# Reordering a ramp on ScalarE, moving a temporary to another buffer pool, and adding seven fp32 matmuls ahead of a cumulative sum

## The chip, the cores and the metric

The kernel runs on one core of a Trainium2 chip. The metric is the device time of one execution in microseconds (us). The kernel before takes 323.64 us in the first set of runs (median of 3, 323.56 to 323.77).

The engines are named as in the profile: PE is TensorE (matmuls), ACT is ScalarE (activation functions and table loads), DVE is VectorE, POOL is GpSimd. Each engine has its own queue of instructions, and in the timelines below what stands behind a waiting instruction in the same queue waits too: in the changed kernel, for instance, one small ScalarE instruction waits 1.46 us for its operand, and the table load behind it starts only at 48.30.

## The reference, cut to what matters

The kernel computes a gated linear recurrence ("gateloop" attention) with a complex decay, and then a gated feed-forward layer on its output.

```python
batch, n_heads, seq, head_dim = (4, 8, 768, 48)
mag = np.sqrt(a_re * a_re + a_im * a_im)
scale = np.minimum(mag, 0.999) / (mag + 1e-06)
a_re_n, a_im_n = (a_re * scale, a_im * scale)
for t in range(S):                        # S_re, S_im: 48 x 48 states for each head
    new_re = ar * S_re - ai * S_im
    new_im = ar * S_im + ai * S_re
    S_re, S_im = (new_re + kv, new_im)    # kv = outer(k_t, v_t)
    y[:, :, t] = np.einsum('bhd,bhde->bhe', q[:, :, t], S_re)
# then, with x = y as 3072 x 384:
gelu = 0.5 * g * (1.0 + erf(g * inv_sqrt2))     # g = x @ w_gate
ffn_out = gelu * (x @ w_val) @ w_out
out = x + res_gate * ffn_out                    # res_gate = sigmoid(x @ w_res)
```

The kernel replaces the loop over time by cumulative sums in log space. For each position it needs the log magnitude of the decay and its angle (an arctan). Both are summed along the sequence by a matmul with a triangular matrix. `exp` of the one and `sin`/`cos` of the other then scale q and k.

## The kernel before

The sequence of each batch is cut into groups of 256 positions, 12 groups in all. They are worked on in units: `[0]`, `[1, 2]`, `[3, 4]`, and so on. "The second unit" is groups 1 and 2, "the third unit" groups 3 and 4. The ramp is the stretch in which the first units' decays are computed while the feed-forward layer has hardly any input yet.

The parts that matter, in the order in which the data pass through them. Comments marked `##` are mine, `...` marks cuts.

```python
    def p1_steps(g):
        def s0():
            ...
            act(out=T["lm", g], in_=T["lm", g], func=AF.Ln)                     ## tile "ar"
        def s1():
            T["s", g] = pS.tile([128, W], FP, tag="s", name="s")                ## pS: 2 buffers
            act(out=T["s", g], in_=T["lm", g], func=AF.Exp, scale=-1.0)
            nc.vector.tensor_tensor(out=T["th", g], in0=T["s", g], in1=T["th", g], op=OP.mult)
        def s2():
            act(out=T["s", g], in_=T["th", g], func=AF.Square)
        def s3():
            act(out=T["s", g], in_=T["s", g], func=AF.Ln, bias=1.0)
            lm = T["lm", g]
            nc.vector.scalar_tensor_tensor(out=lm, in0=T["s", g], scalar=0.5, in1=lm, op0=OP.mult, op1=OP.add)
            nc.vector.tensor_scalar(out=lm, in0=lm, scalar1=LNMAX, scalar2=None, op0=OP.min)   ## "the clamp"
        return [s0, s1, s2, s3]

    def cs_l(g, c):            ## running sum of the log magnitudes; psM: 4 PSUM buffers
        ...
        cs = psM.tile([128, DM], FP, tag="mm", padded_shape=[128, 512], name="csl")
        nc.tensor.matmul(out=cs, lhsT=lmat[c], rhs=T["lm", g][:, sl], start=True, stop=True)
        def ex():              ## "the exponentials": they free the PSUM buffer
            act(out=T["E", g][:, sl], in_=cs, func=AF.Exp)
            act(out=T["Ei", g][:, sl], in_=cs, func=AF.Exp, scale=-1.0)
        return ex

    def cs_t(g, c):            ## running sum of the angles: "cst"
        ...
        cs = psM.tile([128, DM], FP, tag="mm", padded_shape=[128, 512], name="cst")
        nc.tensor.matmul(out=cs, lhsT=tmat[c], rhs=th[:, sl], start=True, stop=(s == 0))
        if s > 0:
            nc.tensor.matmul(out=cs, lhsT=ones2pi, rhs=T["P", g], start=False, stop=True)
        ...                    ## VectorE turns cs into the tile fg (pool pE, 2 buffers); p2_sin takes Sin of it

    def sums(g):               ## per-head sums, for M = exp(sum), the decay over a whole block
        ms = psM.tile([128, H], FP, tag="mm", padded_shape=[128, 512], name="ms")
        two = pS.tile([128, W], FP, tag="s", name="two")
        ...
        for h in range(H):
            nc.tensor.matmul(out=ms[0:DD, h:h + 1], lhsT=two[:, h * DD:(h + 1) * DD], rhs=ones1,
                             start=(h == 0), stop=(h == H - 1), skip_group_check=True)
        T["ms", g] = mp.tile([128, H], FP, tag="ms", name="msb")
        nc.vector.tensor_copy(out=T["ms", g][0:DD], in_=ms[0:DD])
```

The order of all this in the ramp is set by one call of a helper, which sorts steps by a number between 0 and 1:

```python
        if u == 0:             ## g1: second unit, g2: third unit
            sm = [[call(sums, g) for g in gg if g % NS > 0] for gg in (g1, g2)]
            weave((0.0, 0.25, zip_steps([p1(g) for g in g1])), (0.26, 0.3, csls), (0.31, 0.32, sm[0]), (0.35, 0.45, exs),
                  (0.4, 0.64, zip_steps([p1(g) for g in g2])), (0.641, 0.642, dec3), (0.645, 0.65, atn[:1]),
                  (0.65, 0.66, [call(p1_arctan, g) for g in g1]), (0.67, 0.85, cst), (0.75, 0.8, atn[1:]),
                  (0.9, 0.95, sin), (0.96, 0.97, sm[1]), (0.0, 0.5, att))
```

So the queue of ScalarE has, in order: log and exp of the second unit, its exponentials (the last pair behind the first log of the third unit), log and exp of the third unit, the small `M` exponentials, a table load, the arctans, later the sines, another table load, and the GELUs of the feed-forward layer.

## Time and profile before

Over the whole span TensorE is the busiest engine. These are the first line of the page's busy times and the line of its chain that ended last (the share of the span that each engine has in it):

```profile
PE 272.1 (84%) x2200; PEld 170.5 (53%) x2200; DVE 234.8 (73%) x431; ACT 209.8 (65%) x353; POOL 80.5 (25%) x115
PE 56%; SPq 12%; ACT 11%; DMA 9%; DVE 6%; issue 3%; POOL 1%; ACTq 0%; DVEq 0%; POOLq 0%
```

These averages say little about the ramp, where the change lies. The timeline of ScalarE does. Its columns are start in us, duration in us, engine, source line, operation, output and input tile, shapes, count, and in brackets the idle time before with what ended it. L124 is the helper through which every activation goes, so one reads the tile names: E and Ei are the second unit's exponentials, `ar<-ar` the two logs with which the third unit begins, `M<-msb` the block decays, `ai<-ai` the arctans, CS the sines, h the GELUs.

```profile
36.59 0.49 ACT L124 ACTIVATE E<-csl 128x384 f32<-128x384 f32 x1 [0.91 <-PE csl L212]
...
39.52 0.84 ACT L124 ACTIVATE ar<-ar 128x768 f32<-128x768 f32 x1
...
42.05 0.85 ACT L124 ACTIVATE ar<-ar 128x768 f32<-128x768 f32 x1
...
47.74 0.29 ACT L124 ACTIVATE M<-msb 96x8 f32<-96x8 f32 x2
48.05 1.28 ACT L477 ACT_TABLE_LOAD   x1
49.34 3.04 ACT L124 ACTIVATE ai<-ai 128x768 f32<-128x768 f32 x4
57.58 0.94 ACT L124 ACTIVATE CS<-fg,hpi 128x768 bf16<-128x768 f32 x1 [5.20 <-DVE fg L246]
...
65.02 0.66 ACT L124 ACTIVATE h<-gp 128x256 bf16<-128x256 f32 x2
```

The timeline of TensorE in the same stretch (one fp32 matmul is two records, so "x16" are the eight one-column sums of one group and "x2" is one matmul of 384 columns):

```profile
39.21 1.44 PE L296 MATMUL ms<-ones,two 128*96 128x1 f32 x16
...
50.24 1.65 PE L236 MATMUL cst<-ai,lt0b 128*128 128x384 f32 x2 [7.84 <-ACT ai L124]
51.68 1.49 PE L238 MATMUL cst<-P,ones2pi 128*128 128x384 f32 x2
...
56.86 0.81 PE L238 MATMUL cst<-P,ones2pi 128*128 128x384 f32 x2
57.51 1.44 PE L296 MATMUL ms<-ones,two 128*96 128x1 f32 x16
58.81 0.49 PE L439 MATMUL gp<-xT,wg 128*128 128x256 bf16 x3
```

TensorE is idle for 7.84 us before the first cst matmul, and that matmul waits for the arctan. From one start to the next the early cst matmuls take 1.28 us and the late ones 0.65 us, because the granted clock changes between them, from 0.50 to 1.00. The table by windows shows it: after the stretch come busy us (and counts) of PE, PEld, DVE, ACT and POOL, then the granted TensorE clock, the DMA share and GB/s.

```profile
54.00:56.00 2.00, 2.00 (x7) 1.09 (x6) 1.28 (x3) 0.00 (x0) 0.00 (x0) 0.92 1.65 136
64.00:66.00 2.00, 1.11 (x14) 0.86 (x12) 1.86 (x5) 1.67 (x4) 0.00 (x0) 0.64 1.25 233
```

In every clock record of these traces the clock is either 0.5 or 1.0, so a mean of 0.92 in two microseconds tells when it changed. It is low from 44.1 to 54.3 and again from 64.6 to 71.4: by the trace's clock records for 10.24 and for 6.83 us. At the low clock a cst matmul takes 1.28 us against 0.65 us, about twice as long. Below I call what runs at 0.5 cold and what runs at 1.0 warm.

Last, VectorE (`msb` copies the sums out of PSUM, kE is the product of k and Ei, the last line is the clamp of group 4). Later I also name the updates, which are the additions just before the clamps, G and Gb, the running state times M and its bf16 copy, and P, the angle carried over from the group before:

```profile
40.69 0.16 DVE L299 COPY msb<-ms 96x8 f32<-96x8 f32 x1 [1.07 <-PE ms L296]
...
42.72 0.95 DVE L314 TENSOR_TENSOR kE<-k,Ei 128x768 bf16<-128x768 f32 x1
...
51.01 0.55 DVE L198 TENSOR_SCALAR ar<-ar 128x768 f32<-128x768 f32 x1
```

| ramp of the kernel before | us |
|---|---|
| TensorE idle before the first cst | 7.84 |
| first arctan | 49.34 |
| first cst to first Sin | 50.24 to 57.58 |
| first GELU | 65.02 |
| next table load, and the one that opens the last unit | 83.52 and 262.65 |

The last row is a milestone: how late a kernel reaches the same table load says what the ramp cost.

### The profile page before, as it was taken

How to read it: one execution, taken by the hardware profiler on the slowest of the kernel's cores; microseconds unless marked ns; L12 is line 12 of the kernel's file. 1: busy time of each engine (PE TensorE's matmuls, PEld its weight loads, DVE VectorE, ACT ScalarE, POOL GpSimd, SP SyncE). 2: the span in 40 equal slices, each digit the busy share in tenths (PEclk: the TensorE clock that was granted, in tenths of full speed). 3: DMA queues.
4: the chain of work that ended last, by engine and by line, in shares of the span. 5: the costliest groups of instructions: out<-in, count | busy, mean ns of one | idle time of the engine just before them, and what ended most of it. 6: DMA issues, size and time to landing. Idle time of an engine off the chain costs nothing.

```text
span 322.4 us, 5853 instructions
## 1 busy us (share of the span) xinstructions
PE 272.1 (84%) x2200; PEld 170.5 (53%) x2200; DVE 234.8 (73%) x431; ACT 209.8 (65%) x353; POOL 80.5 (25%) x115
## 2 busy tenths in 40 slices
PE   0337927789887999789997999998999999899994
PEld 0116624677543666445664556554656655555682
DVE  2446769968499995599982999974899837864352
ACT  4549684646998557977568976569665683656150
POOL 1206522022040370259020572000630003200220
PEclk9995676959999999999999999999999999999998
DMA  8999999989999995396850595000360003600441
GB/s 159 218 183 181 182 169 165 185 174 180 187 179 186 223 160 33 76 197 113 122 36 2 107 121 95 2 0 3 75 122 3 2 0 76 122 2 0 107 91 50
DMA packets 137755, 34.55 MB, mean 107 GB/s; under 512 B 126848, under 2 KB 137728, under 8 KB 137728
## 3 DMA queue, kind: packets, MB, share of 16 engines
q1 hardware_dynamic: 103296, 23.60, 36.8%
q0 software_dynamic: 34432, 10.59, 31.2%
q8 instruction: 17, 0.28, 0.3%
q14 instruction: 10, 0.08, 0.1%
HBM read 31.31 MB, written 9.07 MB: 125 GB/s over the span
## 4 chain that ended last, share of the span: by engine, by line
PE 56%; SPq 12%; ACT 11%; DMA 9%; DVE 6%; issue 3%; POOL 1%; ACTq 0%; DVEq 0%; POOLq 0%
PE vp L443 14%; PE gp L439 13%; SPq L136 6%; SPq L144 6%; PE op L463 6%; DMA k<-in_k_dram 4%; PE rp L455 3%; PE tp L349 3%; PE tp L346 3%; PE at L356 3%; ACT L477 3%; DMA m<-dm 3%; ACT s L124 3%; PE cst L236 2%; PE y L394 2%
## 5 line engine op out<-in xcount | busy, mean ns | idle before, releaser
L124 ACT ACTIVATE h<-gp 128x512 bf16<-128x512 f32 (+1 forms) x84 | 44.5, 536 | 38.4 <-PE gp L439 37.9
L439 PE MATMUL gp<-xT,wg 128*128 128x512 bf16 (+1 forms) x252 | 65.4, 353 | 3.4 <-ACT h L124 2.0
L443 PE MATMUL vp<-xT,wv 128*128 128x512 bf16 (+1 forms) x252 | 66.6, 353 | 0.0
L446 DVE SCALAR_TENSOR_TENSOR h<-h,vp 128x512 bf16<-128x512 bf16 (+1 forms) x84 | 49.8, 603 | 16.4 <-PE vp L443 12.0
L463 PE MATMUL op<-wo,h 128*128 128x384 bf16 x288 | 50.2, 326 | 8.1 <-ACT Ei L124 5.9
L463 PEld LDWEIGHTS <-h 128*128 128x128 bf16 x288 | 27.8, 98 | 28.7 <-issue 11.3
L351 ACT COPY qk<-tp 96x512 bf16<-96x512 bf16 x48 | 27.9, 580 | 17.1 <-PE tp L349 7.9
L359 DVE TENSOR_TENSOR atm<-at,mask 128x512 bf16<-128x512 f32 x48 | 32.9, 686 | 8.2 <-PE at L356 7.8
L472 POOL DMA_DIRECT2D out_dram<-x x22 | 20.4, 947 | 54.4 <-DMA out_dram<-ot 43.1
L439 PEld LDWEIGHTS <-wg 128*128 128x128 bf16 x252 | 23.7, 99 | 17.9 <-issue 4.2
L443 PEld LDWEIGHTS <-wv 128*128 128x128 bf16 x252 | 23.8, 99 | 13.3
L189 DVE TENSOR_TENSOR ai<-s,ai 128x768 f32<-128x768 f32 x12 | 11.1, 955 | 23.6 <-ACT s L124 23.6
L477 ACT ACT_TABLE_LOAD x21 | 26.9, 1283 | 1.1 <-PEq L615 0.7
L346 PE MATMUL tp<-ident,Q 128*96 128x128 bf16 x192 | 20.1, 231 | 6.9 <-DVE Q L321 6.2
L346 PEld LDWEIGHTS <-Q 128*96 128x96 bf16 x192 | 17.4, 130 | 15.3 <-DVE Q L321 10.0
L124 ACT ACTIVATE CS<-fg,hpi 128x768 bf16<-128x768 f32 x12 | 11.2, 935 | 20.8 <-DVE fg L246 20.7
L150 POOL DMA_DIRECT2D v<-in_v_dram x24 | 21.9, 932 | 4.2 <-DMA v<-in_v_dram 1.3
L349 PE MATMUL tp<-ident,K 128*96 128x128 bf16 x192 | 22.3, 235 | 0.0
L236 PE MATMUL cst<-ai,lt0b 128*128 128x384 f32 x24 | 11.8, 577 | 11.7 <-ACT ai L124 11.0
L352 DVE COPY qk<-tp 96x512 bf16<-96x512 bf16 x48 | 19.8, 413 | 2.3 <-ACT qk L351 1.7
L212 PE MATMUL csl<-ar,lt0a 128*128 128x384 f32 x24 | 11.4, 562 | 10.8 <-DMA ar<-in_a_re_dram 10.8
L466 DVE SCALAR_TENSOR_TENSOR ot<-sg,op 128x384 f32<-128x384 f32 x24 | 13.1, 547 | 10.1 <-PE op L463 10.1
(85 smaller groups left out, 522.0 us busy)
## 6 DMA issues: line engine op xcount, KB each, us to landing
ar<-in_a_re_dram SPq DMA_DIRECT2D x24, 192.0 KB, 4.7
ai<-in_a_im_dram SPq DMA_DIRECT2D x24, 192.0 KB, 4.1
q<-in_q_dram SPq DMA_DIRECT2D x24, 192.0 KB, 3.8
k<-in_k_dram SPq DMA_DIRECT2D x24, 192.0 KB, 3.7
out_dram<-ot SPq DMA_DIRECT2D x24, 192.0 KB, 2.5
out_dram<-x POOLq DMA_DIRECT2D x22, 192.0 KB, 3.7
v<-in_v_dram POOLq DMA_DIRECT2D x24, 96.0 KB, 5.0
wg<-in_moe_w_gate_dram POOLq DMA_DIRECT2D x4, 288.0 KB, 11.4
```

Of the source, the lines that this page charges most:

```text
L124: tab(nc.scalar.activation(**kw))
L150: nc.gpsimd.dma_start(out=t[:, c], in_=rows(v, g, c))
L346: nc.tensor.transpose(out=tp[0:DD, j * 128:j * 128 + 128], in_=Q(x), identity=ident)
L349: nc.tensor.transpose(out=tp[0:DD, 512 + j * 128:640 + j * 128], in_=K(x), identity=ident)
L351: nc.scalar.copy(out=qk[0:DD, 0:512], in_=tp[0:DD, 0:512])
L359: nc.vector.tensor_tensor(out=atm, in0=at, in1=mask4, op=OP.mult)
L439: nc.tensor.matmul(out=gp, lhsT=wg[:, fi, ffi * 128:(ffi + 1) * 128], rhs=xT[:, fi, :], start=(fi == 0), stop=(fi == KD - 1))
L443: nc.tensor.matmul(out=vp, lhsT=wv[:, fi, ffi * 128:(ffi + 1) * 128], rhs=xT[:, fi, :], start=(fi == 0), stop=(fi == KD - 1))
L446: nc.vector.scalar_tensor_tensor(out=h2[:, ffi, :], in0=h2[:, ffi, :], scalar=0.5, in1=vp, op0=OP.mult, op1=OP.mult)
L463: nc.tensor.matmul(out=ps, lhsT=h2[:, ffi, jj * 128:(jj + 1) * 128], rhs=wo[:, ffi, :], start=(ffi == 0), stop=(ffi == KF - 1))
L472: nc.gpsimd.dma_start(out=out[t0:t0 + 128, :], in_=T["x", token(u, jj)], accum_op=OP.add)
L477: tab(nc.scalar.preload_act_table_set(nm))
```

## The change

The intent, as I read it: ScalarE has small gaps between 33 and 41 us; the third unit's log and exp work can fill them if it goes ahead of the second unit's exponentials (all of it except the last logs, `p12[-2:]`, which stay behind them). And if TensorE has something to do in the idle stretch before cst, its clock may be up when cst comes. The whole diff:

```diff
@@ def cs_t(g, c):
         cs = psM.tile([128, DM], FP, tag="mm", padded_shape=[128, 512], name="cst")
+        if g == FIRST + 1 and c == 0:
+            for _ in range(7):
+                nc.tensor.matmul(out=cs, lhsT=tmat[1], rhs=T["lm", NEAR][:, sl], start=True, stop=True)
         nc.tensor.matmul(out=cs, lhsT=tmat[c], rhs=th[:, sl], start=True, stop=(s == 0))
@@ def sums(g):
-        two = pS.tile([128, W], FP, tag="s", name="two")
+        two = pE.tile([128, C * H, 2, D], FP, tag="fg", name="two").rearrange("p x u d -> p (x u d)")[:, 0:W]
@@ in the ramp
-            weave((0.0, 0.25, zip_steps([p1(g) for g in g1])), (0.26, 0.3, csls), (0.31, 0.32, sm[0]), (0.35, 0.45, exs),
-                  (0.4, 0.64, zip_steps([p1(g) for g in g2])), (0.641, 0.642, dec3), (0.645, 0.65, atn[:1]),
+            p12 = zip_steps([p1(g) for g in g2])
+            weave((0.0, 0.25, zip_steps([p1(g) for g in g1])), (0.26, 0.3, csls), (0.31, 0.32, sm[0]), (0.32, 0.5, p12[:-2]),
+                  (0.5, 0.58, exs), (0.6, 0.64, p12[-2:]), (0.641, 0.642, dec3), (0.645, 0.65, atn[:1]),
```

`NEAR` is group 4 and `FIRST + 1` is group 1. The result of the seven matmuls is thrown away, since the next one into the same PSUM buffer has `start=True`. Their operand, the log magnitude of group 4, is ready after the clamp of that group.

## The prediction

> **What bounds the kernel now.** Before takes 323.64 us. The page shows TensorE busy 84% of the span and 56% of the chain that ended last, but the change touches only the ramp, 32 to 72 us, where the latencies of ScalarE, VectorE and TensorE follow each other. In the timeline ScalarE runs Exp and Ln until 47.8, loads a table (1.28 us) and starts the first arctan at 49.34. TensorE is idle from 42.4 to 50.24 (7.8 us, ended by that arctan). Eight fp32 matmuls (cst, 128x384) follow: six at 1.28 us, or less as the clock rises, then 0.65 us each; the last ends at 57.7. VectorE then releases Sin at 57.58, Q starts at 59.53, and the first GELU runs at 65.02. Per-microsecond windows show a granted clock of 0.50 from 44.1 to 54.3 and again from 64.5 to 71.4. [...]
>
> **What the change moves.** ScalarE has small idle gaps from 33 to 41 us (0.84, 0.52, 0.91, 0.25, 0.55 us). The third unit's two Ln and two Exp (about 0.75 us each) fill them; the eight exponentials (0.38 us apart) then run without waits after the squares. Walking the built order with the trace's durations I get the first arctan at about 48.3 instead of 49.34: a gain of about 1 us. Taking the "two" tiles from another pool removes waits for the s buffers.
>
> **What it adds.** Seven fp32 matmuls of 0.65 us (4.5 us) to 1.28 us (9 us). The built order has them directly before the cst matmuls, waiting for the last clamp of the third unit's log magnitudes. On VectorE that clamp stands behind kE, two updates, G, Gb and P. I expect it at 51.5 to 52.1 us, later than the arctan that cst needs, so none of the seven fills the idle 7.8 us: all are on the critical path. They start cold; about four run at 1.28, three at 0.65: some 6.5 to 7 us. Cst then starts near 59 (before: 50.24), all warm (5.2 us, saving about 2), and ends near 64 instead of 57.7.
>
> Second cost: "two" now reuses an fg buffer, so the last sums wait for the first Sin pair, TensorE's gate and value matmuls queue behind those sums, and Q behind their copy: 1 to 2 us more. The first GELU should come near 71 (65.0 before).
>
> Giving back: if the clock stays up, or recovers sooner, after the GELU, up to 2.6 us of the second cold stretch returns. After that, to 102 us, the work is bound by TensorE and then ScalarE, so the delay passes through.
>
> **Sum.** About -1 (ScalarE) +6.7 (seven matmuls) +1.5 (later trigger) -2 (warm cst) +1.5 (fg buffer and order) -1 (later clock) = +5.7 us.
>
> Predicted: 329.3 us, range 325.0 to 333.0. Faster by over 2%: 0.03; within 2%: 0.57; slower by over 2%: 0.40.
>
> **What the profile would show.** Right: Ln of the third unit near 32.6 us; first arctan near 48.3; the extra matmuls starting after the clamp, at 51 to 53, with the first cst matmul waiting for them and not for the arctan; clock 1.0 during cst; the third sums after the first Sin. Wrong: the seven matmuls inside the idle stretch before the arctan, or cst at or before 50.
>
> **What would make it wrong.** [...] the seven run mostly warm, with the clock kept through 72 us: near 325. VectorE reaching the clamp much earlier, so that they overlap the arctan wait: 322 to 324. Or slack later (loads, stores) absorbing the delay.

That about four of the seven would run cold was my estimate; in the trace of before the clock rose 4.1 us after the first cst had begun (50.24 to 54.3), the time of three such matmuls at 1.28 us.

## The result, and the profile after

| | median us | lowest to highest | runs |
|---|---|---|---|
| before | 323.63 | 323.56 to 323.77 | 4 |
| after | 333.51 | 332.11 to 334.66 | 4 |

The ratio is 1.0303 (95% interval 1.0263 to 1.0343): slower by 3%. All these runs are fast (none is over 1.5% above the fastest of its kernel). Here and below a ratio is the mean time of one kernel's fast runs over that of the other's of the same rounds, so it is not quite the ratio of the medians quoted. The profile shown is of the fastest of the four runs after the change, 332.11 us. The median time lies half a microsecond above the predicted range, and the class that I held likeliest (within 2%, 0.57) did not come.

ScalarE after the change:

```profile
32.52 1.58 ACT L124 ACTIVATE ar<-ar 128x768 f32<-128x768 f32 x2
...
41.95 0.47 ACT L124 ACTIVATE E<-csl 128x384 f32<-128x384 f32 x1
...
48.07 0.21 ACT L124 ACTIVATE M<-msb 96x8 f32<-96x8 f32 x1 [1.46 <-DVE msb L302]
48.30 1.28 ACT L480 ACT_TABLE_LOAD   x1
49.59 3.04 ACT L124 ACTIVATE ai<-ai 128x768 f32<-128x768 f32 x4
65.28 0.94 ACT L124 ACTIVATE CS<-fg,hpi 128x768 bf16<-128x768 f32 x1 [12.64 <-DVE fg L249]
...
75.18 0.66 ACT L124 ACTIVATE h<-gp 128x256 bf16<-128x256 f32 x2
```

The third unit's logs start at 32.52 instead of 39.52, as intended. But the second unit's exponentials start at 41.95 instead of 36.59, and the arctan comes no earlier than before (49.59 against 49.34): a new wait of 1.46 us for a small copy on VectorE stands in front of the table load.

TensorE after the change (L238 are the seven matmuls):

```profile
42.85 2.01 PE L299 MATMUL ms<-ones,two 128*96 128x1 f32 x16 [3.47 <-ACT Ei L124]
45.12 2.72 PE L299 MATMUL ms<-ones,two 128*96 128x1 f32 x16 [0.25 <-DVE msb L302]
...
53.60 6.60 PE L238 MATMUL cst<-ar,ut0b 128*128 128x384 f32 x14 [5.42 <-issue]
60.04 0.81 PE L239 MATMUL cst<-ai,lt0b 128*128 128x384 f32 x2
...
68.08 2.69 PE L299 MATMUL ms<-ones,two 128*96 128x1 f32 x16 [2.72 <-DVE two L296]
70.63 0.80 PE L442 MATMUL gp<-xT,wg 128*128 128x256 bf16 x3
```

The seven matmuls do not lie in the stretch before the arctan. They start at 53.60, four microseconds after the first arctan began, and hold the first cst matmul until 60.04. The profile gives their wait to "issue", which here means that it saw no releaser; the clamp on VectorE that makes their operand ends at 52.96 + 0.55 = 53.51. Also new is a gap of 2.72 us before the third group of sums, which then takes 2.69 us instead of 1.44.

VectorE:

```profile
44.90 0.16 DVE L302 COPY msb<-ms 96x8 f32<-96x8 f32 x1 [3.74 <-PE ms L299]
...
47.88 0.16 DVE L302 COPY msb<-ms 96x8 f32<-96x8 f32 x1 [1.91 <-PE ms L299]
...
48.49 0.95 DVE L317 TENSOR_TENSOR kE<-k,Ei 128x768 bf16<-128x768 f32 x1
...
52.96 0.55 DVE L198 TENSOR_SCALAR ar<-ar 128x768 f32<-128x768 f32 x1
...
66.98 0.96 DVE L296 TENSOR_TENSOR two<-ar 128x768 f32<-128x768 f32 x1 [0.21 <-ACT CS L124]
```

It now waits 3.74 and 1.91 us for the sums, so kE comes at 48.49 instead of 42.72 and the clamp at 52.96 instead of 51.01. The last line is the tile `two` of the third sums: it waits for the sine, because it now sits in a buffer of the fg tag.

The clock, by windows (columns as before):

```profile
56.00:58.00 2.00, 2.00 (x5) 1.05 (x4) 0.00 (x0) 0.00 (x0) 0.00 (x0) 0.67 1.32 180
66.00:68.00 2.00, 0.00 (x0) 0.00 (x0) 1.75 (x4) 0.95 (x2) 0.00 (x0) 0.89 0.86 164
74.00:76.00 2.00, 1.34 (x20) 1.25 (x20) 1.27 (x2) 1.14 (x3) 1.31 (x2) 0.90 1.40 235
```

The clock rises at 57.3, falls at 67.6 in the gap of 2.72 us, and rises again at 74.4. The cst matmuls run warm, as was hoped (0.65 us from start to start). The sums (2.69 us), the gate and value matmuls and the first transposes that follow them run cold, at 0.50 until 74.4.

| | before | after | difference |
|---|---|---|---|
| first arctan | 49.34 | 49.59 | +0.25 |
| first cst | 50.24 | 60.04 | +9.80 |
| first Sin | 57.58 | 65.28 | +7.70 |
| first GELU | 65.02 | 75.18 | +10.16 |
| next table load | 83.52 | 91.72 | +8.20 |
| table load of the last unit | 262.65 | 270.64 | +7.99 |

### The profile page after: what moved, and what is told of

Its sections match the earlier page's. It is cut to its first block, busy times and chain, and to the rows that moved or that the text cites. A ratio compares the mean times of both kernels' runs of the same rounds, so it can differ in the third digit from the quotient of the medians.

```text
span 330.3 us, 5853 instructions
## 1 busy us (share of the span) xinstructions
PE 276.2 (84%) x2189; PEld 175.4 (53%) x2214; DVE 233.9 (71%) x431; ACT 209.3 (63%) x353; POOL 81.9 (25%) x115
## 4 chain that ended last, share of the span: by engine, by line
PE 57%; ACT 14%; DVE 11%; DMA 8%; issue 6%; SPq 2%; POOL 1%; DVEq 0%; ACTq 0%; POOLq 0%
PE gp L442 12%; PE vp L446 12%; PE op L466 4%; PE rp L458 4%; PE tp L349 4%; ACT s L124 3%; PE tp L352 3%; PE at L359 3%; ACT L480 3%; DMA m<-dm 3%; PE ms L299 2%; PE cst L239 2%; PE cst L238 2%; PE y L397 2%; PE dk L389 2%
## 5 line engine op out<-in xcount | busy, mean ns | idle before, releaser
L442 PE MATMUL gp<-xT,wg 128*128 128x512 bf16 (+1 forms) x241 | 63.4, 350 | 2.9 <-ACT h L124 1.1
L446 PE MATMUL vp<-xT,wv 128*128 128x512 bf16 (+1 forms) x238 | 61.8, 350 | 0.6 <-DVE ot L469 0.3
L171 POOL COPY landed<-k 1x1 f32<-1x1 f32 x10 | 7.1, 714 | 64.5 <-DMA k<-in_k_dram 64.5
## 6 DMA issues: line engine op xcount, KB each, us to landing
wg<-in_moe_w_gate_dram POOLq DMA_DIRECT2D x4, 288.0 KB, 10.6
```

The source lines that it names most:

```text
L442: nc.tensor.matmul(out=gp, lhsT=wg[:, fi, ffi * 128:(ffi + 1) * 128], rhs=xT[:, fi, :], start=(fi == 0), stop=(fi == KD - 1))
L446: nc.tensor.matmul(out=vp, lhsT=wv[:, fi, ffi * 128:(ffi + 1) * 128], rhs=xT[:, fi, :], start=(fi == 0), stop=(fi == KD - 1))
```

## The experiments

My theory: the loss is made in the ramp. The seven matmuls wait for the clamp of group 4, which lies behind the arctan, so all of them stand before cst; the new buffer of `two` adds a gap that costs the clock; and the new order on ScalarE gains nothing. One rival: the seven are cheap or useful, because they warm the clock for cst, and the order on ScalarE or the buffer makes the loss. Another rival: it is their number that costs, wherever they stand.

All experiments give correct results.

### no_fill: the change without the seven matmuls

```diff
-        if g == FIRST + 1 and c == 0:
-            for _ in range(7):
-                nc.tensor.matmul(out=cs, lhsT=tmat[1], rhs=T["lm", NEAR][:, sl], start=True, stop=True)
```

> The changed kernel without the seven matmuls. Theory 1 (the seven stand on the critical path): the first cst matmul starts with the arctan near 49.6 us, the second waits for P near 53.0, the rest run from there partly at half clock; the second cst group ends near 57, the first Sin near 59.5 instead of 65.3, the time falls by 4 to 6 us to 327.5 to 329.5. Rival (the cost is the moved log/exp work, whose sums run late and on a slow clock, and the seven cost little or help by keeping the clock up): the time stays within 1.5 us of 333.5 or rises.

Measured: 326.76 us (326.52 to 326.83, 4 runs), ratio to before 1.0070 (1.0047 to 1.0093). Taking the seven away gives back some 2.3% of the 3.0%. So the first rival falls: the seven are the larger part of the loss. The time fell even below the 327.5 to 329.5 us expected. But 0.7% (2.3 us) is left. In my sum the parts that stay in this kernel are -1 us for ScalarE and +1.5 us for the buffer. The profile shows where the rest goes, on TensorE:

```profile
45.33 2.72 PE L296 MATMUL ms<-ones,two 128*96 128x1 f32 x16 [0.25 <-DVE msb L299]
50.70 1.65 PE L236 MATMUL cst<-ai,lt0b 128*128 128x384 f32 x2 [2.31 <-ACT ai L124]
53.10 1.65 PE L238 MATMUL cst<-P,ones2pi 128*128 128x384 f32 x2 [0.76 <-DVE P L224]
...
63.38 1.49 PE L296 MATMUL ms<-ones,two 128*96 128x1 f32 x16 [2.62 <-DVE two L293]
```

The second cst matmul waits for P, a sum that stands behind the late kE and clamps in VectorE's queue, and the third sums wait for `two`.

### only_fill: the kernel before with the seven matmuls alone

```diff
         cs = psM.tile([128, DM], FP, tag="mm", padded_shape=[128, 512], name="cst")
+        if g == FIRST + 1 and c == 0:
+            for _ in range(7):
+                nc.tensor.matmul(out=cs, lhsT=tmat[1], rhs=T["lm", NEAR][:, sl], start=True, stop=True)
```

> The kernel before with only the seven matmuls. Theory 1: they start after the third unit's last clamp near 51.6 us, hold cst back to 57.5 to 59 (50.2 before), and the first GELU moves by 5 to 7 us; time 327.5 to 330.5. Rival (the seven cost little): cst all on the full clock and the time within 1.5 us of 323.6.

Measured: 332.40 us (331.53 to 334.10, 4 runs), ratio 1.0252 (1.0213 to 1.0290). With the old order the seven start at 52.50 and the first cst at 58.97. The milestone of the last unit is 6.1 us late (268.76). The profiled run, the slowest of the four, loses another 3.8 us at the end; see "A slow tail" below. The time lies above the 327.5 to 330.5 us expected; without that tail it would lie within (an estimate: 332.4 - 3.8 = 328.6). At the milestone, before the tail, the seven alone cost 6.1 us or 1.9%; taking them out of the change gives back 2.3%.

### only_fg: the kernel before with `two` in an fg buffer alone

```diff
-        two = pS.tile([128, W], FP, tag="s", name="two")
+        two = pE.tile([128, C * H, 2, D], FP, tag="fg", name="two").rearrange("p x u d -> p (x u d)")[:, 0:W]
```

> The kernel before with only the other buffer for two. If the reuse of an fg buffer costs on the critical path: the third sums start after the first Sin pair (near 60 us, 57.5 before), the first Q starts near 61.8 instead of 59.5, the first GELU moves by 1.5 to 2.5 us, time 325 to 326. If the reuse is off the path: the same time within 0.5 us.

Measured: 325.47 us (323.76 to 325.80, 6 runs), ratio 1.0038 (1.0011 to 1.0066), about 1.2 us. The third sums wait 2.72 us for `two` as in the change, but here the cold stretch that follows is short (61.8 to 65.2), and the profiled run, the fastest of the six, is even 0.7 us ahead of before at the last milestone. So this part costs little by itself.

### early_fill12: the kernel before with twelve matmuls that are ready early

```diff
+        if g == FIRST + 1 and c == 0:
+            for _ in range(12):
+                nc.tensor.matmul(out=cs, lhsT=tmat[1], rhs=T["lm", FIRST + 1][:, sl], start=True, stop=True)
```

> The kernel before with twelve matmuls on the second unit's log magnitudes, which are ready at 36.6 us, so they can start in the idle stretch near 42.4 and end near 50.1 at 0.645 us each. If warm filling in the idle stretch is worth anything: the clock stays 1.0 from 37 through 57 us, the eight cst matmuls take 5.2 instead of 7.4 us, the first Sin moves 1.5 to 2 us earlier, and the time is 321.5 to 323. If the clock falls in spite of them or cst is not what Sin waits for: 323.5 or more.

Measured: 325.45 us (325.19 to 327.15, 4 runs), ratio 1.0042 (1.0008 to 1.0077). In the ramp it does what the change meant to do. On TensorE:

```profile
42.12 7.96 PE L238 MATMUL cst<-ar,ut0b 128*128 128x384 f32 x24
50.14 0.91 PE L239 MATMUL cst<-ai,lt0b 128*128 128x384 f32 x2
...
59.36 0.42 PE L349 MATMUL tp<-ident,Q 128*96 128x128 bf16 x4 [1.19 <-DVE Q L324]
```

The twelve fill the idle stretch exactly, all cst matmuls run warm from the first (0.65 us from start to start, the clock at 1.00), and the first GELU comes at 61.94 (before: 65.02). The second rival falls with it in the ramp: twelve matmuls there cost nothing (first cst at 50.14, before: 50.24). But the clock still falls at 61.0, and the gain at the last milestone is 2.4 us only. And the timed kernel is not faster at all (321.5 to 323 us were expected), because in its profile it loses 3.3 us after that milestone.

### fill14: the change with fourteen instead of seven

```diff
-            for _ in range(7):
+            for _ in range(14):
```

> The changed kernel with 14 instead of 7 of the added matmuls. If they stand on the critical path, each further one costs its 0.645 us at full clock: the first cst matmul at about 64.5 us (60.0 with seven), time 333.5 + 4.5 = 337 to 338.5. If a longer burst pays for part of itself by keeping the clock up behind it: less than +3 us.

Measured: 335.10 us (334.19 to 335.37, 4 runs), ratio 1.0333 (1.0308 to 1.0358). The first cst is at 64.79, 4.75 us later than in the change: seven matmuls at full clock, as expected. But the time is only 0.4 to 1.6 us longer than the change's in its two sets. The profile shows the rest given back at once: the clock is low only from 74.7 to 78.1, 3.4 us, and the first GELU comes at 78.36, 3.2 us later than in the change. The slope in the time was a miss. A sum of terms does not hold here: in the two profiles of the change the clock was low for 6.8 and for 10.2 us after cst, and here for 3.4 us.

### early_trigger: the change, the seven on an operand that is ready early

```diff
-                nc.tensor.matmul(out=cs, lhsT=tmat[1], rhs=T["lm", NEAR][:, sl], start=True, stop=True)
+                nc.tensor.matmul(out=cs, lhsT=tmat[1], rhs=T["lm", FIRST + 1][:, sl], start=True, stop=True)
```

> The changed kernel, the same seven matmuls, but on the second unit's log magnitudes, ready since about 36 us, so that only their trigger moves: they start after the transposes of x near 48.1 instead of 53.6. If the late trigger is what costs: cst starts near 55 instead of 60, the time falls by 4 to 6 us to 327.5 to 329.5, near the 326.8 without them. If the matmuls themselves or the clock cost, wherever they start: less than 2 us better than 333.5.

Measured: 328.19 us (327.56 to 328.78, 4 runs), ratio 1.0129 (1.0107 to 1.0151). The same seven matmuls, with the same shapes, start at 48.08:

```profile
48.08 7.37 PE L238 MATMUL cst<-ar,ut0b 128*128 128x384 f32 x14
```

Between this kernel and the change only the trigger differs, and (1.0303 - 1.0129) of 323.7 us is 5.6 us. The late trigger is the largest single part of the loss. What is left, 1.3%, fits what the profile still shows: the second sums end only near 48 and the seven come after them, so the first cst is at 55.28 and the first Sin at 60.52 (before: 57.58); and the gap before the third sums is there, with a low clock for 10.2 us after it (63.6 to 73.8). Even with the early trigger the seven do not pay in this order: no_fill, which has none, stands at 1.0070, in other rounds.

### no_fill_sbuf: the new order without the seven, the third sums' tile back in its old pool

```diff
-        two = pE.tile([128, C * H, 2, D], FP, tag="fg", name="two").rearrange("p x u d -> p (x u d)")[:, 0:W]
+        two = (pE.tile([128, C * H, 2, D], FP, tag="fg", name="two").rearrange("p x u d -> p (x u d)")[:, 0:W]
+               if g <= FIRST + 2 else pS.tile([128, W], FP, tag="s", name="two"))
```

and the seven removed as in no_fill. The new order with every `two` in the old pool could not be run: the third unit's exp waits for an s buffer that the sums on TensorE must release, these wait for a PSUM buffer that the second unit's exponentials release, and those stand behind that exp on ScalarE. A buffer of its own for `two` did not fit in memory, by 64 bytes in each partition (3 kb asked for, 2.9375 kb left). So the move to fg is what makes the new order possible, and only its third use can be undone; "the order alone" below means the new order with the first two uses in fg.

> The changed kernel without the seven matmuls and with the third sums back in the s buffers (the first two stay in fg, without which the order deadlocks). If the fg reuse of the third sums is what is left of the loss beside the seven: the third sums start right behind cst near 60.6 instead of 63.4, Q some 1.5 us earlier, time 325 to 326 (326.8 with it). If the moved log/exp work holds the loss (the late, slow sums delay the chain): still 326.5 to 327.

Measured: 325.04 us (324.47 to 325.98, 4 runs), ratio 1.0035 (1.0010 to 1.0059). The order alone is no gain but a small loss, with the arctan at 49.49. Against no_fill (1.0070) the third sums' buffer costs 0.35%, 1.1 us, when the seven are absent. That agrees with only_fg (1.2 us), but the two ratios come from different rounds and chips, and their difference of 0.35% is hardly more than its own uncertainty of about 0.3%.

### early12_w6: a second look at early_fill12

The label suggests another kernel. What ran is line for line the kernel of early_fill12. It counts as a second profile of that kernel.

> A second look at the early fill of twelve in the kernel before, for how the end of the kernel differs between executions. If the late transfer of the decay factors (3.6 us in the first look, 1.6 in the kernel before) is a matter of chance: about 1.6 and the time near 321.5; if it is tied to this kernel's timing: again 3.2 or more and near 325.3.

Measured: 323.97 us in one run, of unknown state, so the time proves nothing. The profile repeats the first: first GELU at 62.86, last milestone at 259.03 (3.6 us ahead of before), and the same loss after it, 63.1 us to the end.

### after_again and fill7_sbuf: the change again, and the change with the third sums' tile back in its old pool

after_again is the changed kernel, not edited. fill7_sbuf has the edit of no_fill_sbuf, and keeps the seven. They ran on the same chip in the same rounds.

> The changed kernel once more, for the spread between executions and for a second profile. If the first profile (332.1, the fastest of four) is typical of the ramp [...]: first cst matmul at 59.5 to 60.5 us again, time 331.5 to 334.5.

> The changed kernel with its seven matmuls, the third sums back in the s buffers. In the changed kernel TensorE idles 2.7 us behind cst, waiting for the third sums' tile, and the clock falls before the sums, gates and transposes. If the buffer is the cause: the sums follow cst at about 65.4 instead of 68.1, at full clock, the first GELU comes near 72.5 instead of 75.2, time 1 to 2 us less than the changed kernel of these rounds. If the clock would fall anyway: less than 0.7 us.

Measured: after_again 334.66 us (334.41 to 335.08, 4 runs), ratio 1.0317 (1.0286 to 1.0348). fill7_sbuf 330.88 us (330.57 to 331.14, 4 runs), ratio 1.0199 (1.0169 to 1.0229). after_again missed its expectation a little: the first cst is at 61.15 and not at 59.5 to 60.5, and the median is just above the 334.5 us named. With the seven present, the same buffer costs 3.8 us and not 1.1 or the 1 to 2 expected. In fill7_sbuf TensorE goes on from cst to the sums without a gap and warm:

```profile
66.44 1.44 PE L300 MATMUL ms<-ones,two 128*96 128x1 f32 x16
```

In after_again they come at 69.19 and take 2.48 us, and the clock is low for 10.2 us, from 69.4 to 79.7; in fill7_sbuf it is low for 3.4 us, from 72.9. The first GELU is at 76.19 there and at 73.98 in fill7_sbuf, although the first cst is at nearly the same time (61.15 and 61.28).

after_again also shows what two profiles of one kernel can differ by: its milestones are +10.4 and +10.6 us, those of the first profile of the change +8.2 and +8.0. In the first profile the clock rose at 57.3, the seven held cst for 6.44 us, and the cold stretch later was 6.8 us long. In the second it rose at 59.2, the seven held cst for 7.17 us, and the cold stretch was 10.2 us long.

### early12_cs6: early_fill12 with six more matmuls in the second gap

```diff
     def gv_step(u, ffi):
         ...                                   ## after the value matmuls
+        if u == 0 and ffi == 1:
+            wy = psY.tile([128, 512], FP, tag="y", name="wy")
+            cw = T["CS", gs(1)[0]].rearrange("p x u d -> p (x u d)")[:, 0:512]
+            for _ in range(6):
+                nc.tensor.matmul(out=wy, lhsT=ident, rhs=cw, start=True, stop=True)
```

(with the twelve early matmuls of early_fill12)

> The kernel before with twelve early matmuls and six more (512 columns, of the first Sin's output) in the idle time before the second unit's transposes, to keep the clock up there too. If that idle time is what drops the clock near 61: it stays 1.0 through 68 us, the first table load after the second GELU stage comes 4.5 to 5.5 us earlier than in the kernel before (83.5), time 319 to 322. If the clock drops in spite of them: near the 324 to 325.5 of the twelve alone. If late transfers at the end eat the gain: the lead is there until 260 us and gone at 300.

Measured: 319.71 us (319.07 to 321.57, 6 runs), ratio to before 0.9862 (0.9833 to 0.9892). This version beats both kernels. The six take their operand from the first sine, which is ready before the gap: one runs at 58.52, ahead of the last value matmuls, and most of them from 59.28 to 60.31, where the gap was. The windows of early_fill12 and, after it, of this kernel, in the stretch where the former loses its clock:

```profile
60.00:62.00 2.00, 1.11 (x18) 1.05 (x18) 2.00 (x4) 1.97 (x4) 0.00 (x0) 0.74 1.29 191
62.00:64.00 2.00, 2.00 (x14) 1.44 (x13) 2.00 (x5) 0.98 (x4) 0.00 (x0) 0.50 1.25 185
```

```profile
60.00:62.00 2.00, 1.39 (x18) 0.98 (x17) 2.00 (x4) 1.98 (x3) 0.00 (x0) 1.00 1.28 184
62.00:64.00 2.00, 1.29 (x14) 0.99 (x14) 2.00 (x4) 1.69 (x5) 0.00 (x0) 1.00 1.27 186
```

The clock stays at 1.0 here; no stretch of one us from 38 to 90 shows less. The last milestone is at 259.05, 3.6 us ahead of before, and this kernel has no slow tail (the next section but one). What follows is that the eighteen fillers together, ready when the idle time begins, are worth 1.4% here. How much of the difference from early_fill12 the six make by themselves is not settled, since most of it is the tail: the second profile of early_fill12, whose clock did fall (from 62.8 to 66.2), reached the same milestone at 259.03.

### reorder_warm: the new order with early fillers around the first sums

```diff
-            for _ in range(7):
-                nc.tensor.matmul(out=cs, lhsT=tmat[1], rhs=T["lm", NEAR][:, sl], start=True, stop=True)
+            for _ in range(6):
+                nc.tensor.matmul(out=cs, lhsT=tmat[1], rhs=T["lm", FIRST + 1][:, sl], start=True, stop=True)
     def sums(g):
+        if g == FIRST + 1:
+            wa = psA.tile([128, 4, 128], FP, tag="at", name="wa").rearrange("p j t -> p (j t)")[:, 0:DM]
+            for _ in range(6):
+                nc.tensor.matmul(out=wa, lhsT=tmat[1], rhs=T["lm", g][:, 0:DM], start=True, stop=True)
```

(with the third sums' tile in the old pool)

> The changed order without its seven matmuls, third sums in s, but six matmuls before the first sums (from about 39.5 us) and six behind them, all on values that are ready, so that TensorE stays on the full clock through 57 us. If slow sums are what ate the gain of the moved log/exp work: the sums end near 46 instead of 47.7, the table load comes at 46.7 instead of 48.2, P near 51, all cst at full clock, cst ends near 56 (60.1 without), first GELU near 62.5, time 320.5 to 323. If the order itself loses (VectorE's queue): cst no earlier than in the early fill of twelve (50.1) and the time above its 324 to 325.

Measured: 326.23 us (325.49 to 327.03, 4 runs), ratio 1.0048 (1.0013 to 1.0084). The sums now run warm (1.44 us from 44.47), and cst runs warm (the clock at 1.00 until 63.3). But the arctan is still at 49.44 and P at 52.18, and the first GELU at 63.94 is later than early_fill12's 61.94. So warm sums did not rescue the new order here. But the test is not clean: the six fillers in front of the sums run from 40.52 to 44.64, so the first sums start 1.6 us later than in the change (42.85), and the second end at 47.68, hardly before the 47.84 of the change. VectorE again gets the sums late and then has kE, updates, G, Gb and P to do one after the other. Warm sums that start on time were not tried. The last milestone, 260.88, is 1.8 us ahead of before, but behind early_fill12's 260.21 without the new order; the rest of the time is the tail of the next section.

### A slow tail, not explained

Three kernels (only_fill, early_fill12 in both looks, reorder_warm) lose 3.3 to 4.5 us, against before, after the last milestone: from there to the end of the span they take 63.0 to 64.2 us, all others 59.2 to 59.8. On the chain of waits one small transfer (1.5 KB of decay factors) is slow. In before, and in early_fill12:

```profile
265.20 1.60 DMA dm<-Ei
```

```profile
262.75 3.56 DMA dm<-Ei
```

TensorE runs out of work behind it (0.59 us busy of the three from 272 to 275) and its clock falls as well, from 276.0 to 279.4. How much of the loss is the transfer and how much the clock is not shown. The first look names the transfer, but why it is slow at this place in those three kernels and not in the others no run here tells: the same transfer for an earlier unit, at 181.54, takes 3.43 us in before too. It is left open. It does not touch the change itself, whose tail is as short as before's (330.3 - 270.64 = 59.7 us against 322.4 - 262.65 = 59.8 us).

## Why the prediction was wrong

The main mechanism that I named is what the runs show: the seven wait for group 4's clamp, later than the arctan, and all of them are on the critical path; cst runs warm; `two` in an fg buffer makes the third sums wait for the sine. What failed are sizes. The terms of my sum against the first profile of the change:

| step | predicted us | measured us | from |
|---|---|---|---|
| ScalarE: arctan earlier | -1 | +0.25 | 49.34 to 49.59 |
| seven matmuls | +6.7 | +6.44 (second profile: +7.17) | 53.60 to 60.04; 53.98 to 61.15 |
| later trigger | +1.5 | +3.11 (the rest of the next line) | |
| sum of these: first cst | +7.2 | +9.80 (second profile: +10.91) | 50.24 to 60.04; 61.15 |
| warm cst | -2 | -2.10 | first cst to first Sin, 7.34 to 5.24 |
| fg buffer and order | +1.5 | +2.46 | first Sin to first GELU, 7.44 to 9.90 |
| later clock | -1 | -2.17 | +10.16 at the GELU, +7.99 at the last milestone |
| total | +5.7 | +7.99 | last milestone |

**The step that failed: "a gain of about 1 us" on ScalarE, and the trigger "at 51.5 to 52.1 us".** The arctan came 0.25 us later instead, and the clamp ended at 53.51. By the waits in the profile they are one error. I had walked ScalarE's queue with the durations of before, and let the sums on TensorE take what they took there. But the exponentials that I moved back also release the four PSUM buffers of csl, and the sums need one. In before the first sums start at 39.21. After the change they wait for the first pair of exponentials until 42.85. TensorE is idle for 3.47 us, its clock falls at 43.7, and the two groups of sums take 2.0 and 2.7 us instead of 1.44 and 1.50. The copy to VectorE is late, and from there the delay goes two ways. It goes to ScalarE: the 1.46 us wait of `M` stands before the table load, and without it the arctan would have come at 49.59 - 1.46 = 48.13, near my 48.3. And it goes down VectorE's queue: kE, the updates and the clamp, so that the seven start at 53.60. no_fill_sbuf isolates the order, though not this chain within it: the order alone costs 0.35% where I had a gain.

**The sum did not even add up to the text.** The text has the first cst "near 59", 8.8 us after before's 50.24. The three terms in the sum make 7.2. I counted a gain on ScalarE of 1 us that the clamp, and no longer the arctan, made worthless: once the seven wait for VectorE, an earlier arctan moves nothing. Taken from the text alone the prediction would have been about 1.5 us higher, and a range shifted with it would have reached 334.5 us, above the median measured.

**The term for the fg buffer was mis-sized with the seven present.** It costs 1.1 us without them, within the "1 to 2 us" that I gave, and 3.8 us with them. The gap before the third sums is 2.6 to 2.7 us either way. What differs is how long the clock is low after it: without the seven 3.4 us in no_fill_sbuf and 6.8 us in no_fill, 3.4 us more; with them 3.4 us in fill7_sbuf and 10.2 us in after_again, 6.8 us more. Half of 6.8 us is 3.4 us, an estimate of what that much more time at the low clock (1.28 us for a cst matmul against 0.65 us) costs work that TensorE bounds, and the runs of that pair differ by 3.8 us. In the first profile of the change the low clock lasted 6.8 us, 3.4 us more than in fill7_sbuf.

**What was right.** The seven's own time (6.5 to 7 predicted, 6.44 and 7.17 measured), warm cst (5.2 us, as predicted), Ln of the third unit at 32.52 (32.6 predicted), and, in the first profile, the clock's recovery after the GELU, 2.2 us (up to 2.6 predicted, 1 put into the sum). That last one was partly luck: in the second profile only 0.6 us came back (76.19 against 65.02 at the GELU, 273.27 against 262.65 at the last milestone).

The steps of the change, by ratio to before: new order 1.0035, with the seven 1.0199, with the third sums' buffer as well 1.0303 and 1.0317 in two sets. The first and the second step were timed in different rounds, on different chips, each against before.

The spread is part of the answer. The four runs of the change lie 2.55 us apart and its two profiles 2.6 us at the last milestone, and with them the clock changes at different times (it rose at 57.3 and at 59.2). My range of 8 us was wide enough for that, and its centre was wrong.

## What to carry to other kernels

A filler that is to keep TensorE's clock up must depend on data that are ready when the idle time begins: here the twelve that started at 42.12 kept it at 1.0 through cst. The one that waited for something later than the work it should warm moved that work back, by its own length and by its wait (first cst 9.80 us later). Before an engine's work is reordered, ask what each moved instruction releases (here PSUM buffers), and follow that release through every in-order queue behind it, with durations at the clock that will then be granted (here 2.0 and 2.7 us for the two groups of sums and not 1.44 and 1.50). When the trigger of a critical step moves to another engine, gains on the old engine no longer count.

## What is left open about the clock

- What makes the clock fall. In the change it fell at 67.6, in a single gap of 2.72 us on TensorE; in early_fill12 at 61.0, after two gaps of 1.19 and 0.45 us close together. But in after_again it stayed at 1.0 through a gap of 3.41 us and fell only at 45.5, 1.8 us after TensorE had work again (43.73). So the length of one gap does not tell it by itself.
- What the clock is worth. It falls again in the middle of the work: two profiles of one kernel differ by 2.6 us of 330 (0.8%) at the last milestone, with 3.4 us more of low clock after cst in the slower, and the kernel whose clock stays up through the ramp is 1.4% faster than before. How much of the 1.4% is the clock by itself is not isolated.
